# One score matmul per head and block of 32 steps, laid into the score matrix by plain copies

## The chip, the cores and the metric

The kernel runs on one core of one Trainium2 chip. The metric is the device time of one execution in microseconds (us). The version before the change took 1008.17 us, the median of three runs (1007.17 to 1009.46 us).

## The reference

The reference chains three parts. First a linear attention with decay: for each of 4 batches and 8 heads a 48 x 48 state is carried over 768 steps,

```python
cur = einsum('bhd,bhe->bhde', u * k_t, v_t)
y_t = einsum('bhd,bhde->bhe', r_t, state + cur)
state = w_t[..., None] * state + einsum('bhd,bhe->bhde', k_t, v_t)
```

Its output, 3072 tokens of 384 values, goes through a gated feed-forward layer, (sigmoid(x Wg) * (x Wv)) Wo with 1536 hidden units, and that through a second one, mish(x Wi) Wo2 with 2048 hidden units. Everything is float32 with a tight tolerance, so each large product is made of three float16 matmuls (high times high, high times low, low times high).

## The kernel before

**The attention.** Time is cut into blocks of C = 32 steps, and two blocks make a pair; there are 24 blocks (`j`) and 12 pairs (`p`). Inside a block the recurrence becomes a 32 x 32 score matrix per head: the entry (s, t) is the key of step s times the receptance (`r`) of step t, with the decays of the steps between them. The block's output is scores times values plus the decayed `r` times the state that the block starts from.

- `fine(p)` makes the scores inside groups of eight steps, on GpSimd (POOL) and VectorE (DVE), and leaves `r`, `k` and `w` scaled by the decays inside each group.
- `coarse(p, cells)` makes the scores between the four groups of eight of a block. It transposes `k`, `r` and `w` into KD, RD and WD (L573, L567, L580; one tile holds all 32 heads of both blocks), and lets TensorE (PE) form the scores in two levels (L602). The first level, 64 matmuls with 32 x 24 outputs, takes every group's keys against the receptances of the groups from 1 on; then KD's first group and RD's groups 1 and 3 are multiplied by one group's decay each (three `scaled`, L612), and the second level, 64 matmuls with 16 x 16 outputs, writes again over the places where groups 0 and 1 meet groups 2 and 3. A fourth `scaled` prepares RD for the product with the state. The tile X gets the fine scores by a transpose (L618), and `merge` lays the coarse scores over them by one predicated copy with a mask (L625).
- `keys(p)` prepares the keys for the state, transposed into KT (L661).
- `step(j)` multiplies scores and values, and RD and state, into one PSUM tile `yp` (L687), splits it into float16 parts (L204, L207), sends them transposed to `xt`, and updates the state: decay (L763), outer products `kp` (L790), join (L801).

The PSUM tiles `lp` (scores), `yp` and `kp` share three banks of 2 KB each in rotation (`next_at`): a tile can be written once the tile three allocations earlier has been read.

**The feed-forward layers.** `gate(p, f)` and `out1(p, c, part)` are the first layer, on the 256 tokens of a pair: 18 matmuls of 256 columns per `gate` (L835), whose result is multiplied by its sigmoid on ScalarE (ACT) and DVE (L846, L851, L863, L866), and 9 per `out1` part (L899). `h_unit` and `out2` are the second layer (L1020, L1065), which starts when the attention is over. The weights arrive as raw 64-bit words and are decoded to two float16 parts by ACT, DVE and POOL (`decode_early` and `decode`: L275, L286, L297, L300, L351, L362, L375): those of the first layer in the first 130 us, `wi` and `wp` of the second around 535 to 620 us.

**What sets the order.** All work is added as tasks to a `Plan`, with an engine (or several to choose from), an estimated cost and the keys it reads and writes. `Plan.run` is a list scheduler: it keeps a clock per engine by these costs, ranks tasks by how late they may be, and writes each engine's instructions in the order that comes out. Tasks marked `burst` (the small attention matmuls) are kept at least SPACE = 1.9 apart by that clock. On the chip every engine runs its queue in order and waits on semaphores, so a late result on one engine holds everything that stands behind the waiting instruction.

Of the kernel before, what the change touches and what calls it, by code (L numbers as in the profile page):

```python
# [19 lines left out]
NP = NJ // 2  # L20
BH = B * H
HG = BH // 2
DP = 32
BLK = C * (DH + DP + DH)
DM = H * D
KC = DM // 128
# [125 lines left out]
def mixer_moe_kernel(  # L152
# [12 lines left out]
    nc = tc.nc  # L165
# [27 lines left out]
    mask = ap.tile([128, 2, C], F32, name="mask")  # L193
# [202 lines left out]
    xp = {}  # L396
    rd = {}
    kd = {}
    wd = {}
    lps = {}  # L400
# [154 lines left out]
    def coarse(p, cells):  # L555

        R, K, W = (("blk", p % 2, i) for i in range(3))
        RD, KD, WD, X = ("RD", p % 2), "KD", ("WD", p % 2), ("X", p % 2)
        bank = next_at()

        def window(o, step, n):
            v = blk[p][:, o : o + step]
            return bass.AP(v.tensor, v.offset, [list(v.ap[0]), [step, n], [1, 32]])

        def flip_r(e):
# [24 lines left out]

        def level(n, part):
            for i in range(8 * part, 8 * part + 8):
                for e in range(2):
                    for g in range(2):
                        o = 64 * g + 32 * e
                        x = HG * e + i
                        gs = slice(64 * g, 64 * g + 64)
                        if n == 8:
                            m, out, rhs = C, lps[p][o : o + 32, i, 8:], rd[p][gs, x, 8:]
                        else:  # L600
                            m, out, rhs = 16, lps[p][o : o + 16, i, 16:], rd[p][gs, x, 16:]
# [4 lines left out]
        def level8(e):  # L606
            lps[p] = pp.tile([128, HG, C], F32, tag=f"at{bank[1]}", name=f"lp{p}")
            level(8, 0)

        def scaled(e, t, w):  # L610
            shape = [128, BH, t.shape[-1]]
            engines[e].tensor_tensor(  # L612
                out=t, in0=t, in1=w.unsqueeze(2).to_broadcast(shape), op=ALU.mult
            )

        def flip_a(e):
            xp[p] = ap.tile([128, BH, C], F32, tag=f"X{p % 2}", name=f"X{p}")
            nc.vector.transpose(  # L618
                out=xp[p].rearrange("p x t -> p t x"),
                in_=A[:, :1024].rearrange("p (t s) -> p t s", s=C),  # L620
            )

        def merge(e):
            full = [128, 2, HG, C - 8]
            nc.vector.copy_predicated(  # L625
                out=xp[p].rearrange("p (e i) t -> p e i t", e=2)[:, :, :, 8:],
                mask=mask[:, :, 8:].bitcast(U32).unsqueeze(2).to_broadcast(full),
                data=lps[p][:, :, 8:].unsqueeze(1).to_broadcast(full),
            )

        attn("dve", 2.0, flip_k, [K], [KD])
        attn("dve", 2.0, flip_r, [R], [RD])
        attn("dve", 1.9, flip_w, [W], [WD])
        attn("pe", 0.7, level8, [RD, KD], [bank], burst=True)
        attn("pe", 0.7, lambda e: level(8, 1), [RD, KD], [bank], burst=True)
        both = {"dve": 0.8, "pool": 1.05}
        attn(both, 0, lambda e: scaled(e, kd[p][:, :, :8], wd[p][:, 1]), [WD], [KD])
        attn(both, 0, lambda e: scaled(e, rd[p][:, :, 24:], wd[p][:, 2]), [WD], [RD])
        attn(both, 0, lambda e: scaled(e, rd[p][:, :, 8:16], wd[p][:, 0]), [WD], [RD])
        for part in range(2):  # L640
            attn("pe", 0.7, lambda e, n=part: level(16, n), [RD, KD], [bank], burst=True)
        attn({"dve": 1.2, "pool": 1.7}, 0, lambda e: scaled(e, rd[p][:, :, 16:], wd[p][:, 4]), [WD], [RD])
        attn("dve", 2.0, flip_a, [*cells], [X])
        attn("dve", 1.0, merge, [bank, "mask"], [X])

    def keys(p):
        R, K, W = (("blk", p % 2, i) for i in range(3))
# [23 lines left out]
    def step(j):  # L671
        p, e = divmod(j, 2)
        V = ("v", j % 3)
        S, nxt = ([("s", i % 2, x) for x in range(2)] for i in (j, j + 1))
        ybank = next_at()

        def rows_out(part):
            if not part:
                yps[j] = pp.tile([128, 512], F32, tag=f"at{ybank[1]}", name=f"yp{j}")
            for h in range(4 * part, 4 * part + 4):  # L680
                for n in range(2 if j else 1):
                    for b in range(B):
                        g = b // 2
                        gs = slice(64 * g, 64 * g + 64)
                        i = b % 2 * H + h
                        x = HG * e + i
                        nc.tensor.matmul(  # L687
                            yps[j][32 * b : 32 * b + 32, h * D : h * D + D],
                            (rd if n else xp)[p][gs, x, :],
                            (ss if n else vs)[j][gs, i, :],  # L690
                            start=(n == 0),
                            stop=(n == 1 or j == 0),
                        )
# [31 lines left out]
        for part in range(2):  # L725
            attn(
                "pe",
                0.8 * (COLD if j < 4 else 1.0),
                lambda _, part=part: rows_out(part),
                [("X", p % 2), ("RD", p % 2), V, *S],  # L730
                [ybank],
                burst=True,
            )
        xs = ("xs", j % 2)
# [376 lines left out]
            fill=0.0,  # L1111
        )

    def masks(e):

        nc.gpsimd.memset(mask, 0.0)
        for i in range(4):
            m = mask[32 * i : 32 * i + 32, i % 2]
            nc.gpsimd.memset(m, 1.0)
            nc.gpsimd.affine_select(  # L1120
                out=m,
                in_=m,
                pattern=[[8, C // 8], [0, 8]],
                base=0,
                channel_multiplier=-1,
                compare_op=ALU.is_gt,
                fill=0.0,
            )

    add("act", 1.3, lambda e: nc.scalar.preload_act_table(AF.Sigmoid), [], ["table1"])  # L1130
    add("dve", 0.2, consts, [], ["consts"])
    attn("dve", 1.3, lambda e: nc.vector.memset(A, 0.0), [], ["A"])
# [47 lines left out]
            decode(("wp", i), dst, (2, DM), i, slot, ["open"], W2HI, W2LO)  # L1180

    cells = {0: fine(0)}
    attn("pool", 2.0, masks, [], ["mask"])
    tail1(0)
    tail2(0)
    cells[1] = fine(1)
# [86 lines left out]
```

## Time and profile before

| | |
|---|---|
| median of 3 runs | 1008.17 us |
| span of the profiled execution | 1008.4 us |
| PE busy | 937.8 us (93%) |
| DVE busy | 521.2 us (52%) |
| ACT busy | 345.9 us (34%) |
| POOL busy | 309.8 us (31%) |
| share of the chain that ended last, PE | 81% |
| share of it on L602, the score matmuls | 2% |

The chain that ended last is followed back from the last instruction: at each step to what released it, or to the instruction before it on its engine. Busy shares over the whole span hide that the kernel has stretches with different limits: the start with the weight decoding, a long regular stretch in which one pair of attention blocks and one pair of gate work repeat, a transition with the second layer's weights, and the second layer alone. The runs' median and the profiled span differ by 0.02%.

### The profile page before, as it was taken

What the parts mean: (1) busy time and instruction counts of PE and PEld (TensorE: products, weight loads), DVE (VectorE), ACT (ScalarE), POOL (GpSimd) and SP (SyncE); (2) the same over time, 40 slices, a digit from 0 to 9 for tenths busy, and PEclk for the clock granted to TensorE, in tenths of its full rate; (3) what the DMA queues carried; (4) which work ended last, traced back from release to release, by engine and by line L of the source; (5) the groups of instructions that cost most, each with busy time, mean ns of one, the idle gap of its engine ahead of it and who ended that gap; (6) DMA issues with size and microseconds to landing.
All of it is one profiled execution on the core that took longest, in us unless ns stands there. A gap on an engine that the chain in (4) does not pass through costs nothing.

```text
span 1008.4 us, 32823 instructions
## 1 busy us (share of the span) xinstructions
PE 937.8 (93%) x14952; PEld 678.7 (67%) x14952; DVE 521.2 (52%) x830; ACT 345.9 (34%) x692; POOL 309.8 (31%) x324
## 2 busy tenths in 40 slices
PE   0277889999999999999999999999999999999998
PEld 0266778888888888888888787655555555555555
DVE  5898887666675757666679666221111111111110
ACT  3346723222222222222225466443333333333320
POOL 8871383726264553626274111000000000000000
PEclk9998889999999999999999999999999999999999
DMA  9354625131322214132213460010100101000000
GB/s 307 119 167 154 208 75 133 41 86 48 88 41 81 58 62 97 34 87 54 73 36 116 140 202 12 11 45 8 48 8 17 47 8 48 16 9 17 8 16 32
DMA packets 56475, 72.12 MB, mean 72 GB/s; under 512 B 20752, under 2 KB 37648, under 8 KB 56208
## 3 DMA queue, kind: packets, MB, share of 16 engines
q1 hardware_dynamic: 39696, 66.09, 21.7%
q10 hardware_dynamic: 16640, 3.94, 2.1%
q8 instruction: 117, 1.92, 0.8%
q14 instruction: 22, 0.18, 0.1%
HBM read 56.64 MB, written 9.44 MB: 66 GB/s over the span
## 4 chain that ended last, share of the span: by engine, by line
PE 81%; DVE 9%; DMA 5%; ACT 2%; issue 1%; ACTq 1%; SPq 0%; POOL 0%; DVEq 0%
PE gv L835 23%; PE o L1065 19%; PE h L1020 18%; PE o L899 12%; PE yp L687 3%; PE kp L790 3%; PE lp L602 2%; DMA raw_wv<-wv 2%; DMA raw_wg<-wg 1%; DVE A L483 1%; DVE word_wi L286 1%; DMA raw_wp<-wo 1%; DVE word_wi L275 1%; DMA raw_wo<-wo 1%; DVE X L618 1%
## 5 line engine op out<-in xcount | busy, mean ns | idle before, releaser
L1020 PE MATMUL h<-x,wis 128*128 128x512 f16 x864 | 201.5, 379 | 0.0
L835 PE MATMUL gv<-xt,wgs 128*128 128x256 f16 x1296 | 165.6, 275 | 4.3 <-DVE gt L866 3.7
L899 PE MATMUL o<-gt,wos 128*128 128x256 f16 x1296 | 165.5, 273 | 3.2 <-DVE xo L207 3.2
L835 PE MATMUL gv<-xt,wvs 128*128 128x256 f16 x1296 | 166.3, 274 | 0.0
L462 POOL TENSOR_TENSOR blk<-blk 128x384 f32<-128x384 f32 (+1 forms) x144 | 128.8, 907 | 60.2 <-DVE WD L580 31.6
L1020 PEld LDWEIGHTS <-wis 128*128 128x128 f16 x864 | 84.5, 98 | 90.7
L899 PEld LDWEIGHTS <-wos 128*128 128x128 f16 x1296 | 126.6, 98 | 21.7 <-issue 4.1
L835 PEld LDWEIGHTS <-wgs 128*128 128x128 f16 x1296 | 124.2, 98 | 22.0 <-issue 4.8
L835 PEld LDWEIGHTS <-wvs 128*128 128x128 f16 x1296 | 120.8, 98 | 17.9
L846 ACT ACTIVATE sig<-gv 128x256 f32<-128x256 f32 x144 | 55.0, 383 | 226.4 <-PE gv L835 222.9
L1031 ACT ACTIVATE e<-h 128x512 f32<-128x512 f32 x96 | 57.3, 597 | 207.5 <-PE h L1020 207.5
L462 POOL TENSOR_TENSOR pt<-blk 128x384 f32<-128x384 f32 (+1 forms) x96 | 104.9, 1119 | 45.6 <-DMA blk<-rkw 44.1
L851 DVE SCALAR_TENSOR_TENSOR gv<-gv,sig 128x256 f32<-128x256 f32 x144 | 61.9, 431 | 67.7 <-ACT sig L846 67.2
L866 DVE TENSOR_TENSOR gt<-gv,gt 128x256 f16<-128x256 f32 x144 | 60.4, 419 | 36.4 <-ACT gt L863 36.4
L863 ACT CAST gt<-gv 128x256 f16<-128x256 f32 x144 | 53.3, 372 | 72.0 <-DVE gv L851 57.0
L602 PE MATMUL lp<-RD,KD 64*16 64x16 f32 (+1 forms) x3072 | 34.9, 185 | 40.8 <-DVE RD L567 34.1
L602 PEld LDWEIGHTS lp<-RD,KD 64*16 64x16 f32 (+1 forms) x3072 | 30.1, 101 | 50.4 <-DVE RD L567 34.1
L1038 DVE SCALAR_TENSOR_TENSOR wos<-e,wos 128x512 f16<-128x512 f32 x27 | 18.7, 692 | 84.5 <-ACT wos L1034 84.5
L1065 PE MATMUL o<-wps,wgs 128*128 128x384 f16 x324 | 58.5, 326 | 0.0
L1065 PE MATMUL o<-wps,wos 128*128 128x384 f16 x324 | 57.2, 326 | 0.0
L1038 DVE SCALAR_TENSOR_TENSOR wgs<-e,wgs 128x512 f16<-128x512 f32 x27 | 18.7, 692 | 73.8 <-ACT wgs L1034 73.8
L483 DVE TENSOR_REDUCE A<-pt 128x32 f32<-128x768 f32 (+1 forms) x60 | 51.3, 862 | 0.8 <-POOL pt L462 0.8
(91 smaller groups left out, 1065.3 us busy)
## 6 DMA issues: line engine op xcount, KB each, us to landing
v<-vt SPq DMA_DIRECT2D x96, 96.0 KB, 3.0
blk<-rkw SPq DMA_DIRECT2D x22, 384.0 KB, 3.8
raw_wi<-wi SPq DMA_DIRECT2D x8, 768.0 KB, 4.9
raw_wp<-wo SPq DMA_DIRECT2D x8, 768.0 KB, 5.2
blk<-rkw SPq DMA_DIRECT2D x11, 512.0 KB, 4.4
raw_wg<-wg SPq DMA_DIRECT2D x6, 768.0 KB, 4.6
raw_wv<-wv SPq DMA_DIRECT2D x6, 768.0 KB, 5.8
raw_wo<-wo SPq DMA_DIRECT2D x6, 768.0 KB, 5.6
```

Of the source, the lines that this page charges most:

```text
L462: engines[e].tensor_tensor(out=pv, in0=a, in1=b, op=ALU.mult)
L483: nc.vector.tensor_reduce(out=cell(), in_=shape(pts.pop(n)), op=ALU.add, axis=AX.X)
L602: nc.tensor.matmul(out, kd[p][gs, x, :m], rhs, start=True, stop=True, skip_group_check=True)
L835: nc.tensor.matmul(gps[p, f][:, o], w[:, a, kc, fs], xt[p][:, c, kc, :], start=(n == 0), stop=(n == 3 * KC - 1),)
L846: nc.scalar.activation(out=sgs[p, f], in_=gps[p, f][:, 0], func=AF.Sigmoid, scale=1.0 / (SW * SX))
L851: nc.vector.scalar_tensor_tensor(out=gps[p, f][:, 1], in0=gps[p, f][:, 1], scalar=SG / (SW * SX), in1=sgs.pop((p, f)), op0=ALU.mult, op1=A ...
L863: nc.scalar.copy(out=gt[p][:, 0, f], in_=gps[p, f][:, 1])
L866: nc.vector.tensor_tensor(out=gt[p][:, 1, f], in0=gps[p, f][:, 1], in1=gt[p][:, 0, f], op=ALU.subtract,)
L899: nc.tensor.matmul(ops[p, c][:, :NT], wos[:, a, f, cs], gt[p][:, g, f, :], start=(f == 0 and n == 0), stop=(f == NF1 - 1 and n == 2),)
L1020: nc.tensor.matmul(hps[r, f], w2["wi"][:, a, kc, fs], x2[r][:, c, kc, :], start=(n == 0), stop=(n == 3 * KC - 1),)
L1031: nc.scalar.activation(out=es[r, f], in_=hps[r, f], func=AF.Mish, scale=ih)
L1065: nc.tensor.matmul(ops2[r, t][:, :DM], g2[r][f][:, c, tsl], w2["wp"][:, a, f, :], start=(f == 0 and n == 0), stop=(f == NF2 - 1 and n == 2),)
```

## The change

RD becomes wider: 56 columns per head instead of 32 (`RC`), seven groups of eight. Groups 0 to 3 hold what they held; groups 4 and 6 get copies of steps 16 to 23 and 24 to 31 as they leave `fine`, and group 5 gets steps 24 to 31 times one group's decay. `flip_r` fills it by two transposes of half the size (steps 0 to 15 into groups 0 and 1, steps 16 to 31 into groups 4 and 6); two `scaled` then make group 5 from group 6 (256 elements per partition) and groups 2 and 3 from 4 and 5 (512). With that, groups 1 to 6 hold every scaling of `r` that any group of keys needs, and KD is no longer scaled. One matmul per head and block, with all 32 key columns against 48 columns of RD and a 32 x 48 output, gives all scores: 64 per pair instead of 128, in two bursts of 32 (one for each block `e`), each into a PSUM bank of its own. So `coarse` takes two banks of the rotation instead of one.

From the 48 columns the valid ones are laid into X by plain copies from PSUM, `merge(on, e, n)`: for each block `e` and each 32-partition quarter `n` three copies, from 24, 16 and 8 partitions with 8 x 8, 8 x 16 and 8 x 24 elements per partition; a later one overwrites what an earlier one laid on too many rows. That makes 8 tasks and 24 copies per pair, on ACT or DVE as the planner chooses, in place of one predicated copy of 768 elements per partition. The mask and the 9 POOL instructions that made it go away. Last, RD's groups 1 to 3 are multiplied for the product with the state by one `scaled` of 768 elements, after the scores (before: one of 512 after the second level, groups 1 and 3 having been scaled between the levels). `step` waits for the four merges of its own block only. The scratch memory for dynamic DMA is set to 1024 bytes, which makes room for RD's two larger buffers.

```diff
-        bank = next_at()
+        X = [[("X", p % 2, e, n) for n in range(4)] for e in range(2)]
+        banks = [next_at() for _ in range(2)]
...
-            rd[p] = ap.tile([128, BH, C], F32, tag=f"RD{p % 2}", name=f"RD{p}")
-            nc.vector.transpose(
-                out=rd[p].rearrange("p x t -> p t x"), in_=window(0, DH, C)
-            )
+            if not half:
+                out = rd[p][:, :, :16].rearrange("p x t -> p t x")
+            else:
+                out = rd[p].rearrange("p x (b t) -> p b t x", t=8)[:, 4:7:2]
+            nc.vector.transpose(out=out, in_=window(16 * DH * half, DH, 16))
...
-        def level(n, part):
...
+        def scaled(e, to, of, n, w):
+            engines[e].tensor_tensor(
+                out=rd[p][:, :, 8 * to : 8 * (to + n)],
+                in0=rd[p][:, :, 8 * of : 8 * (of + n)],
+                in1=wd[p][:, w].unsqueeze(2).to_broadcast([128, BH, 8 * n]),
...
+        def scores(e):
+            lps[p, e] = pp.tile([128, 8, RC - 8], F32, tag=f"at{banks[e][1]}", name=f"lp{p}_{e}")
+            for i in range(8):
+                for q in range(2):
                     for g in range(2):
-                        o = 64 * g + 32 * e
-                        x = HG * e + i
+                        o = 64 * g + 32 * q
+                        x = HG * e + 8 * q + i
...
                         nc.tensor.matmul(
-                            out, kd[p][gs, x, :m], rhs, start=True, stop=True, skip_group_check=True
+                            lps[p, e][o : o + 32, i], kd[p][gs, x], rd[p][gs, x, 8:], start=True, stop=True
                         )
...
-        def merge(e):
-            full = [128, 2, HG, C - 8]
-            nc.vector.copy_predicated(
...
+        def merge(on, e, n):
+            put = nc.scalar.copy if on == "act" else nc.vector.tensor_copy
+            xs = slice(HG * e + 8 * (n % 2), HG * e + 8 * (n % 2) + 8)
+            for a, c in ((2, 40), (1, 24), (0, 0)):
+                rs = slice(32 * n, 32 * n + 8 * (a + 1))
+                t = 8 * (a + 1)
+                put(out=xp[p][rs, xs, t:], in_=lps[p, e][rs, :, c : c + C - t])
...
+        both = {"dve": 0.55, "pool": 0.9}
+        attn(both, 0, lambda e: scaled(e, 5, 6, 1, 2), [WD], [(*RD, 2)])
+        attn({"dve": 0.85, "pool": 1.35}, 0, lambda e: scaled(e, 2, 4, 2, 1), [WD, (*RD, 2)], [(*RD, 1)])
+        parts = [(*RD, n) for n in range(3)]
+        for e in range(2):
+            attn("pe", 0.85, lambda _, e=e: scores(e), [*parts, KD], [banks[e]], burst=True)
+        attn("dve", 2.0, flip_a, [*cells], X[0] + X[1])
+        for e in range(2):
+            for n in range(4):
+                attn({"act": 0.8, "dve": 0.9}, 0, lambda on, e=e, n=n: merge(on, e, n), [banks[e]], [X[e][n]])
+        attn({"dve": 1.2, "pool": 1.9}, 0, lambda e: scaled(e, 1, 1, 3, 0), [WD], [(*RD, 1)])
```

The order on PE around the scores of pair 8, in the regular stretch, before. A row is an instruction by its line, with output and inputs (`gv7_4` is gate 4 of pair 7, `o16_1` a part of the first layer's output, `kp16_0` the outer products and `yp16` the output of block 16), its size and, behind an x, how many stand in a row.

```order
L602 MATMUL lp8_7133<-RD8_6794,KD8_6738 32x24 x32
...
L835 MATMUL gv7_4_7171<-xt7_6673,wgs_88 128x256
...
L899 MATMUL o16_1_7184<-gt6_6153,wos_90 128x256
...
L602 MATMUL lp8_7133<-RD8_6794,KD8_6738 16x16 x32
...
L790 MATMUL kp16_0_7368<-v16_6083,KT_92 32x48 x32
...
L687 MATMUL yp16_7431<-v16_6083,X8_6671 32x48 x4
```

And the same place on PE after the change.

```order
L611 MATMUL lp8_0_6805<-RD8_6418,KD8_6529 32x48 x32
...
L837 MATMUL gv7_4_6843<-xt7_6284,wgs_88 128x256
...
L901 MATMUL o16_1_6863<-gt6_5865,wos_90 128x256
...
L611 MATMUL lp8_1_6877<-RD8_6418,KD8_6529 32x48 x32
...
L792 MATMUL kp16_0_6947<-v16_5744,KT_92 32x48 x32
...
L689 MATMUL yp16_7011<-v16_5744,X8_6595 32x48 x4
```

Before, four `lp` bursts of 32 stand there (two of each size), with one or two pieces of 9 gate or output matmuls between them; after, two. In both orders the outer products `kp16_0` come before `yp16`. After the change they stand four pieces of 9 and the burst `lp8_1` behind `lp8_0`, and three banks in rotation give `kp16_0` the bank of `lp8_0`.

DVE at the same place, before: the last scaling of RD and the predicated copy.

```order
L866 TENSOR_TENSOR gt7_7038<-gv7_3_7096,gt7_7038 128x256
L612 TENSOR_TENSOR RD8_6794<-RD8_6794,WD8_6857 128x32x8 x2
L851 SCALAR_TENSOR_TENSOR gv7_4_7171<-gv7_4_7171,sig_7249 128x256
L866 TENSOR_TENSOR gt7_7038<-gv7_4_7171,gt7_7038 128x256
L851 SCALAR_TENSOR_TENSOR gv7_5_7238<-gv7_5_7238,sig_7306 128x256
L866 TENSOR_TENSOR gt7_7038<-gv7_5_7238,gt7_7038 128x256
L612 TENSOR_TENSOR RD8_6794<-RD8_6794,WD8_6857 128x32x16
L625 COPY_PREDICATED X8_6671<-mask_94,lp8_7133 128x32x24
```

DVE at the same place, after.

```order
L853 SCALAR_TENSOR_TENSOR gv7_3_6767<-gv7_3_6767,sig_6838 128x256
L628 COPY X8_6595<-lp8_0_6805 24x8x8
L628 COPY X8_6595<-lp8_0_6805 16x8x16
L628 COPY X8_6595<-lp8_0_6805 8x8x24
...
L868 TENSOR_TENSOR gt7_6710<-gv7_3_6767,gt7_6710 128x256
L483 TENSOR_REDUCE A_91<-pt_6779 128x16
L628 COPY X8_6595<-lp8_1_6877 24x8x8
...
L853 SCALAR_TENSOR_TENSOR gv7_4_6843<-gv7_4_6843,sig_6945 128x256
L803 TENSOR_TENSOR s17_6465<-kp16_0_6947,s17_6465 128x384
```

Six copies follow `lp8_0` on DVE and six `lp8_1`; ACT has as many, in front of and behind the cast of `gv7_3`. In pairs 3 to 9 the copies are split 12 and 12, and all scaling of RD stands on POOL, where DVE had three of the four. In pairs 0 to 2 ACT has 48 copies and DVE 24, and DVE two of the scalings (512 and 768 elements; before, three of 256, and two more decays of the state); in pair 11 ACT has 15 and DVE 9, and POOL all scalings.

## Rows read from the trace of the kernel before

**Rows 1.** Stretches: us; busy PE, PEld, DVE, ACT, POOL (x instructions); clock; DMA.
```profile
0.00:137.00 137.00, 74.94 (x2193) 61.78 (x2197) 114.51 (x177) 65.80 (x119) 87.14 (x100) 0.92 0.57 181
...
534.00:625.00 91.00, 85.83 (x1314) 71.89 (x1313) 67.70 (x104) 54.92 (x101) 23.27 (x13) 1.00 0.43 129
...
137.00:534.00 397.00, 396.97 (x9364) 339.88 (x9354) 272.49 (x454) 97.32 (x257) 199.40 (x212) 1.00 0.26 68
```

**Rows 2.** The chain that ended last, one period: start us, us, what.
```profile
259.47 2.95 PE gv L835 x27
...
305.20 2.95 PE gv L835 x27
...
316.01 0.98 PE gv L835 x9
316.99 0.67 PE lp L602 x50
317.67 1.09 PE gv L835 x9
...
322.48 0.62 PE lp L602 x51
323.10 1.09 PE gv L835 x9
...
330.75 0.81 PE yp L687 x64
331.56 1.09 PE gv L835 x9
```

**Rows 3.** Groups by form: PE matmuls of attention: form, count, busy us, mean ns.
```profile
L602 PE MATMUL lp<-RD,KD 64*32 64x24 f32 x1536 | 18.1, 192 | 34.9 <-DVE RD L567 34.1 <-DVE WD L580 0.8
...
L687 PE MATMUL yp<-s,RD 64*32 64x48 f32 x1472 | 40.0, 212 | 1.6 <-DVE s L801 1.6
```

**Rows 4.** Groups by form on ACT, DVE and POOL.
```profile
L204 ACT ACTIVATE xo<-o 128x256 f16<-128x256 f32 x36 | 13.8, 383 | 11.9 <-PE o L899 11.9
L204 ACT ACTIVATE xs<-yp 128x384 f16<-128x384 f32 x24 | 11.7, 490 | 31.2 <-PE yp L687 31.2
L207 DVE SCALAR_TENSOR_TENSOR xo<-o,xo 128x256 f16<-128x256 f32 x36 | 15.1, 418 | 4.2 <-ACT xo L204 3.5
L207 DVE SCALAR_TENSOR_TENSOR xs<-yp,xs 128x384 f16<-128x384 f32 x24 | 13.1, 546 | 0.9 <-ACT xs L204 0.9
L612 DVE TENSOR_TENSOR RD<-RD,WD 128x256 f32<-128x256 f32 x20 | 13.1, 688 | 11.6 <-PE lp L602 11.6
L612 DVE TENSOR_TENSOR RD<-RD,WD 128x512 f32<-128x512 f32 x9 | 11.0, 1222 | 0.0
L612 POOL TENSOR_TENSOR RD<-RD,WD 128x512 f32<-128x512 f32 x3 | 3.2, 1065 | 5.2 <-PE lp L602 5.2
L625 DVE COPY_PREDICATED X<-mask,lp 128x768 f32<-128x768 uint32 x12 | 12.0, 999 | 0.0
L763 DVE TENSOR_TENSOR s<-s,WD 128x384 f32<-128x384 f32 x11 | 7.3, 667 | 0.0
```

**Rows 5.** Waits of PE, 40 to 137 us: who for whom, us in total, times, longest.
```profile
PE yp L687 <- DVE X L625: 5.9, 2, 3.2
PE kp L790 <- issue: 5.7, 3, 3.5
```

**Rows 6.** The chain that ended last, in the transition.
```profile
552.64 0.77 DVE RD L612
...
553.74 0.91 DVE RD L612
...
560.78 2.05 DVE RD L612
562.83 0.94 DVE X L625
...
563.81 0.88 PE yp L687 x64
```

More of the change, by code (lines that the diff above doesn't have):

```diff
@@ L23 @@
 DP = 32
+RC = 56
 BLK = C * (DH + DP + DH)
@@ L192, in mixer_moe_kernel @@
     U = ap.tile([128, DH], F32, name="U")
-    mask = ap.tile([128, 2, C], F32, name="mask")
     engines = {"dve": nc.vector, "pool": nc.gpsimd}
@@ L557, in coarse @@
         R, K, W = (("blk", p % 2, i) for i in range(3))
-        RD, KD, WD, X = ("RD", p % 2), "KD", ("WD", p % 2), ("X", p % 2)
-        bank = next_at()
+        RD, KD, WD = ("RD", p % 2), "KD", ("WD", p % 2)
+        X = [[("X", p % 2, e, n) for n in range(4)] for e in range(2)]
+        banks = [next_at() for _ in range(2)]
         def window(o, step, n):
@@ L563, in window, with flip_r @@
             return bass.AP(v.tensor, v.offset, [list(v.ap[0]), [step, n], [1, 32]])
-        def flip_r(e):
-            rd[p] = ap.tile([128, BH, C], F32, tag=f"RD{p % 2}", name=f"RD{p}")
-            nc.vector.transpose(
-                out=rd[p].rearrange("p x t -> p t x"), in_=window(0, DH, C)
-            )
+        def flip_r(e, half):
+            if p not in rd:
+                rd[p] = ap.tile([128, BH, RC], F32, tag=f"RD{p % 2}", name=f"RD{p}")
+            if not half:
[3 more added lines that the diff above has]
+            nc.vector.transpose(out=out, in_=window(16 * DH * half, DH, 16))
         def flip_k(e):
@@ L589, in flip_w @@
                 )
-        def level(n, part):
-            for i in range(8 * part, 8 * part + 8):
-                for e in range(2):
+        def scaled(e, to, of, n, w):
[3 more added lines that the diff above has]
+                in1=wd[p][:, w].unsqueeze(2).to_broadcast([128, BH, 8 * n]),
+                op=ALU.mult,
+            )
+        def scores(e):
+            lps[p, e] = pp.tile([128, 8, RC - 8], F32, tag=f"at{banks[e][1]}", name=f"lp{p}_{e}")
+            for i in range(8):
+                for q in range(2):
                     for g in range(2):
-                        o = 64 * g + 32 * e
-                        x = HG * e + i
+                        o = 64 * g + 32 * q
+                        x = HG * e + 8 * q + i
                         gs = slice(64 * g, 64 * g + 64)
[L598 to L601, printed above, removed]
                         nc.tensor.matmul(
-                            out, kd[p][gs, x, :m], rhs, start=True, stop=True, skip_group_check=True
+                            lps[p, e][o : o + 32, i], kd[p][gs, x], rd[p][gs, x, 8:], start=True, stop=True
                         )
[L606 to L614, printed above, removed]
         def flip_a(e):
@@ L621, in flip_a @@
             )
-        def merge(e):
-            full = [128, 2, HG, C - 8]
-            nc.vector.copy_predicated(
[L626 to L629, printed above, removed]
+        def merge(on, e, n):
[5 more added lines that the diff above has]
+                put(out=xp[p][rs, xs, t:], in_=lps[p, e][rs, :, c : c + C - t])
@@ L631, in coarse @@
         attn("dve", 2.0, flip_k, [K], [KD])
-        attn("dve", 2.0, flip_r, [R], [RD])
+        attn("dve", 1.1, lambda e: flip_r(e, 0), [R], [(*RD, 0), (*RD, 1)])
+        attn("dve", 1.1, lambda e: flip_r(e, 1), [R], [(*RD, 2)])
         attn("dve", 1.9, flip_w, [W], [WD])
[L634 to L644, printed above, removed]
+        both = {"dve": 0.55, "pool": 0.9}
@@ L673, in step @@
         V = ("v", j % 3)
+        X = [("X", p % 2, e, n) for n in range(4)]
+        RD = [("RD", p % 2, n) for n in range(2)]
         S, nxt = ([("s", i % 2, x) for x in range(2)] for i in (j, j + 1))
@@ L688, in rows_out @@
                             yps[j][32 * b : 32 * b + 32, h * D : h * D + D],
-                            (rd if n else xp)[p][gs, x, :],
+                            (rd if n else xp)[p][gs, x, :C],
                             (ss if n else vs)[j][gs, i, :],
@@ L729, in step @@
                 lambda _, part=part: rows_out(part),
-                [("X", p % 2), ("RD", p % 2), V, *S],
+                [*X, *RD, V, *S],
                 [ybank],
@@ L1112, in unit @@
         )
[L1114 to L1128, printed above, removed]
     add("act", 1.3, lambda e: nc.scalar.preload_act_table(AF.Sigmoid), [], ["table1"])
@@ L1182, in mixer_moe_kernel @@
     cells = {0: fine(0)}
-    attn("pool", 2.0, masks, [], ["mask"])
     tail1(0)
@@ L1261 @@
     }
-    nc = bacc.Bacc("TRN2", target_bir_lowering=False, num_devices=1)
+    nc = bacc.Bacc(
+        "TRN2", target_bir_lowering=False, num_devices=1, dynamic_dma_scratch_size=1024
+    )
     args = [
```

## Prediction

> **What bounds the kernel now.** I read busy time by stretch first, because the shares over the whole span mix four regimes [rows 1]. [...] In the transition, 534 to 625, PE waits some 5 us; after that the second layer is PE alone. [...]
>
> The second view is the chain that ended last, in one period of the long stretch [rows 2]. The reader is to see that it is PE without a break, and what a burst of small matmuls costs in it: its own piece, and 0.11 us by which the piece of 9 gate matmuls behind it is longer (1.09 for 0.98). A first-level score burst is 0.67 + 0.11 = 0.78 us, a second-level one 0.62 + 0.11 = 0.73, a `yp` burst 0.81 + 0.11 = 0.92. The third view gives the shapes [rows 3]: `yp` from RD is K = 64, 32 weight columns, 48 moving columns in float32, on the same four tiles of the array. That is exactly the new score matmul, so its price need not be guessed.
>
> **The change part by part.**
>
> *PE in the long stretch.* Per pair two bursts of each level go, 2 x (0.78 + 0.73) = 3.02 us, and two of the new shape come, 2 x 0.92 = 1.84. That is 1.18 us less per pair. The score bursts of pairs 3 to 10 lie between 137 and 534 us, 8 pairs: 9.4 us. Two bounds, since no score burst of this size is in the trace: were the price set by the number of matmuls alone, the new bursts would cost 2 x 0.78 and the gain 8 x 1.46 = 11.7 us; were it set by the moving columns alone (48 for 24), 4 x 0.78 = 3.12, a loss of 0.8 us. The `yp` row is the same operation, so I take 9.4.
>
> [...] The bursts show about 12 ns per matmul instruction (0.78 us for 64 of them, two to a float32 matmul). [...]
>
> *The copies.* A copy from PSUM costs, by the splitting of `yp` and `o`, 490 ns for 384 elements and 383 for 256 on ACT, and 546 and 418 on DVE [rows 4]: 0.84 and 1.0 ns per element on about 165 ns. Copies of 64, 128 and 192 elements are then some 0.22, 0.28 and 0.33 us: 0.83 us per merge task on ACT, 0.87 on DVE. Partition counts of 8 to 24 are not in the trace. Ends: 24 copies at 0.165 us each, 4 us per pair, and 24 at the 999 ns of the predicated copy, 24 us. I take the line through the two points, 12 copies on each engine: ACT +3.3 us per pair, DVE +3.5. DVE gives up the predicated copy (1.0) and, in pairs 3 to 9, three scalings (0.69, 0.69, 1.22), so its load hardly grows; ACT goes from some 11 to some 14 us of a period of 45. What hides them is the PE stretch itself: neither engine is near its limit there.
>
> [...] ACT's 490 ns at 384 elements is what one long copy costs. [...]
>
> *The waits that the change adds.* `kp` of the first block now takes the bank of `lp_0` and so waits for its four merges. Behind it in PE's queue stand the gates and `yp`. From the end of `lp_0` it comes after two pieces of 9, `lp_1`, and two pieces: 1.09 + 0.98 + 0.81 + 1.09 + 0.98 = 4.95 us. In that time ACT and DVE each lay two merges, 1.7 us, behind at most a sigmoid, a product or a reduction. So there are about 2 to 3 us of slack. `yp` needs RD's last scaling, on POOL (512 elements 1065 ns [rows 4], so 768 some 1.6), after `lp_1`; four pieces and `kp` stand between. Cost nothing, as long as this cover holds.
>
> *The transition.* Pair 11's scores stand among the decoding of `wi`, and there the chain runs through DVE [rows 6]: three scalings, 0.77 + 0.91 + 2.05, and the predicated copy, 0.94, before `yp`. These 4.7 us leave DVE; three merge tasks, 2.6, come. Between a gain of 3.3 us (2.1 on DVE and 1.2 on PE) and a loss of 1.5 us (the last scaling, now on POOL among the weights' subtractions, arrives late) I take a gain of 1.0, since other DVE work fills part of the room.
>
> *The start.* Pairs 0 to 2 lie where DVE is 84% busy. It gets 8 merge tasks, 7.0 us, for three predicated copies, 3.0, and scalings of 512 and 768 elements (1.22 and, by the same slope, 1.75) for three of 256 (2.1): +4.9 us, less two decays at 0.67 [rows 4], +3.6. ACT gets 16 tasks, 13 us on 66, in the queue that decodes the weights. On the other side PE waited 5.9 us for merged X and 5.7 on issue in `kp` [rows 5], two rounds of scaling between PE and the others become one, and the mask is gone from POOL. Ends: all the added DVE work and a third of that again for ACT, +5; most of the wait for X won back, -4. I take +1.5.
>
> *Sum.* -9.4 - 1.0 + 1.5 = -8.9 us on a span of 1008.4. The median of the runs, 1008.17, is the span within 0.02%, so the time becomes 1008.2 - 8.9 = 999.3 us.
>
> **The rivals.**
>
> *The start eats half.* DVE, at 84%, and ACT's in-order queue push the decoding and everything behind it by 5 us, and the transition gives nothing: 1008.2 - 9.4 + 5 = 1003.8. For it: DVE's load there. Against it: PE's 5.9 us of waits for X.
>
> *The start gains too.* The start wins 4 and the transition 3.3: 1008.2 - 9.4 - 7.3 = 991.5. For it: one round of scaling less on a path PE waited on. Against it: DVE has more to do there, not less.
>
> *No gain on PE.* The burst goes by its moving columns: a loss of 0.8, with the start's 1.5 and the transition's 1.0, 1009.5. The `yp` row speaks against it.
>
> *The merges come late (slower).* Place: `kp` of the first block waiting for `lp_0`'s bank in each of the 8 periods, all of PE's queue behind it. If a tiny copy costs as much as the predicated copy, 1.0 us, six in a row are 6 us on each engine behind about 1.5 of other work: 7.5 against 4.95, 2.5 us a period, +20 against -9.4, so 1008.2 + 10.6 + 0.5 = 1019. It decides from a merge task of about 1.7 us (no stall up to there); at 2.3 the gain is gone. The row's line gives 0.85, half of that.
>
> *The bursts don't shrink.* Excluded by the order, which has two bursts of 32 for four.
>
> **How the numbers follow.** My forecast 0.62, alone with a range of 995 to 1003; the start eats half 0.15; the start gains too 0.08; no gain 0.06; late merges 0.09. What can be told from no change is about 0.2%, 2 us. Faster by more than that (below 1006.2): the first three, 0.85; within: most of the fourth, 0.06; slower: the fifth, 0.09. The range that holds 8 in 10 takes in the forecast, the start's loss and half of its gain: 993 to 1006.
>
> **What would show it.** Right: the period of the long stretch falls from 45.73 us (259.47 to 305.20, the same place in successive periods [rows 2]) to about 44.5, PE stays busy all of it, an `lp` piece in the chain reads 0.81 with 1.09 behind it, and copies read 0.2 to 0.35 us. Wrong: waits of `kp` for ACT or DVE copies in the long stretch (late merges); a `lp` piece near 1.4 (no gain); the first saturated microsecond of PE moved from 137 to 142 or to 133 (the start).

## The result and the profile after

The changed kernel takes 1012.59 us (median of 4 runs, 1010.85 to 1013.97) against 1007.67 of the kernel before (4 runs): ratio 1.0051, 95% interval 1.0034 to 1.0068. It is half a per cent slower. The prediction was 999.3 us, 993 to 1006, with 0.85 on faster: wrong in sign and outside its range.

Where it went is read by the start of the same gate matmuls in both traces (first matmul of a pair's gates, before against after, each counted from its span's start). At pair 2, the end of the start, after is 0.54 us late; at pair 10, the end of the regular stretch, 1.15; at the second layer's first matmul, 2.85, and the spans end 2.85 apart. So the start cost 0.5, the stretch 0.6 and the transition 1.7, and the second layer is unchanged. The medians differ by 4.9 us and not by 2.85, mostly because the profiled execution of before was a long one: times lie 1.7 us above spans (the after execution whose span is 1011.3 took 1013.02), so a span of 1008.4 stands for about 1010.1, 2.4 above the median. Where those 2.4 us lie is not shown.

The page of after: busy time of each engine, then two groups of line, operation and shape (busy us, mean ns, idle before).

```profile
PE 929.9 (92%) x13416; PEld 672.2 (66%) x13416; DVE 528.8 (52%) x936; ACT 383.8 (38%) x855; POOL 317.7 (31%) x322
...
L611 PE MATMUL lp<-RD,KD 64*32 64x48 f32 x1536 | 23.3, 216 | 37.0 <-POOL RD L596 37.0
...
L628 ACT COPY X<-lp 24x64 f32<-24x64 f32 x162 | 41.4, 255 | 33.2 <-DVE X L628 25.5
```

The stretches of [rows 1] again, in the same columns. In the long one PE is no longer busy throughout, 389.26 of 397 where it was 396.97; the waits in the next view name 7.4 of the 7.7 us. The second row is the transition: its granted clock is 0.96, where before had 1.00.

```profile
137.00:534.00 397.00, 389.26 (x8367) 334.17 (x8359) 283.88 (x537) 121.57 (x361) 210.66 (x222) 1.00 0.25 68
...
534.00:625.00 91.00, 85.02 (x1184) 72.30 (x1182) 65.19 (x110) 57.16 (x115) 17.27 (x10) 0.96 0.43 129
```

PE's waits in the long stretch (who for whom, us in total, times, longest). Before it had none there.

```profile
PE yp L689 <- DVE s L803: 3.5, 4, 1.3
PE o L901 <- DVE xo L207: 3.3, 5, 0.9
PE yp L689 <- DVE RD L596: 0.6, 1, 0.6
```

The chain that ended last, half a period (start us, us, what), against [rows 2]:

```profile
317.89 0.81 PE lp L611 x64
318.70 1.09 PE gv L837 x9
...
320.77 0.81 PE lp L611 x64
...
329.43 0.81 PE yp L689 x64
330.24 1.10 PE gv L837 x9
...
331.37 0.39 ACT sig L848
331.76 1.46 ACTq L723
...
333.31 1.22 ACTq L723
...
334.57 0.38 ACT gt L865
...
334.98 0.42 DVE gt L868
335.40 0.86 DVE A L483
336.26 0.48 DVE s L803
...
336.78 0.79 PE yp L689 x54
```

The reader is to see two things. The new score burst costs 0.81 with 1.09 behind it, exactly the forecast. And the chain leaves PE: from 331.4 to 334.5 it stands in ACTq, ACT's own instruction queue, which is issuing the two DMA transposes of `xt` (L723); behind them wait ACT's cast of the next gate, DVE's subtraction that needs the cast, a reduction and the state's join (`s`, L803), and for the join PE's next `yp` burst. The same place in ACT's timeline (start us, us, instruction, idle before it and what ended that):

```profile
331.43 3.10 ACTq L723 DMA_TRANSPOSE xt<-xs  x2
334.57 0.37 ACT L865 CAST gt<-gv 128x256 f16<-128x256 f32 x1 [2.83 <-DMA xt<-xs]
```

The releaser named there is the transposes' issue: ACT had been free for 2.83 us with the cast next in its queue.

The transition loses twice. PE's longest wait there, and its part of the chain (start us, us, what):

```profile
PE o L901 <- DVE xo L207: 4.4, 1, 4.4
```

```profile
572.55 6.02 DMA xt<-xs
...
578.77 4.64 DMA raw_wp<-wo
...
584.31 0.38 ACT xo L204
...
584.72 0.43 DVE xo L207
...
585.19 2.08 PE o L901 x9
587.27 3.71 PE gv L837 x18
```

PE waits 4.4 us for the `xo`, and then runs 27 matmuls in 5.79 us, where 27 took 2.95 in the chain of before [rows 2]. From 584 to 591 us the granted clock is 0.52 (0.99 from 578 to 584, 1.00 from 591 to 595). So the wait is followed by 2.8 us that no view of waits shows.

The copies by form (count, busy us, mean ns): 201 to 309 ns on ACT and 223 to 357 on DVE, near the forecast (0.22 to 0.33).

```profile
L628 ACT COPY X<-lp 8x192 f32<-8x192 f32 x54 | 16.7, 309 | 1.7
L628 DVE COPY X<-lp 8x192 f32<-8x192 f32 x42 | 15.0, 357 | 1.4
...
L628 ACT COPY X<-lp 24x64 f32<-24x64 f32 x54 | 10.9, 201 | 29.8 <-DVE X L628 25.5 <-PE lp L611 3.2 <-DVE X L617 0.5
...
L628 DVE COPY X<-lp 24x64 f32<-24x64 f32 x42 | 9.4, 223 | 27.8 <-ACT X L628 26.4 <-PE lp L611 1.1
```

But the two engines don't lay them side by side. One bank's four merges in the timeline: each waits for the other engine's.

```profile
318.77 0.83 ACT L628 COPY X<-lp 24x64 f32<-24x64 f32 x3 [0.40 <-PE lp L611]
319.63 0.92 DVE L628 COPY X<-lp 24x64 f32<-24x64 f32 x3 [0.98 <-ACT X L628]
320.58 0.83 ACT L628 COPY X<-lp 24x64 f32<-24x64 f32 x3 [0.98 <-DVE X L628]
321.44 0.96 DVE L628 COPY X<-lp 24x64 f32<-24x64 f32 x3 [0.90 <-ACT X L628]
```

A bank's merges take 3.6 us, and not the 1.7 that the prediction counted. Over the whole program DVE's copies wait 26.4 us for ACT's, in 31 waits, and ACT's 25.5 for DVE's, in 22. Whether two engines could read one bank without the turns is not shown: no run here tries it.

Last, DVE's queue around the held cast, two pairs after the chain above, in the order in which the program puts it (instruction, tile written, tiles read). Before:

```
504 L618 STREAM_TRANSPOSE X9_7556<-A_91 128x32x32
505 L801 TENSOR_TENSOR s17_6843<-kp16_1_7561,s17_6843 128x384
...
509 L866 TENSOR_TENSOR gt7_7038<-gv7_8_7528,gt7_7038 128x256
```

After:

```
585 L868 TENSOR_TENSOR gt7_6710<-gv7_6_7045,gt7_6710 128x256
586 L803 TENSOR_TENSOR s17_6465<-kp16_1_7134,s17_6465 128x384
```

Before, the gate product that sits behind the transposes' issue (`gv7_8`) came after the join of the state; in after the held product (`gv7_6`) comes just ahead of it; in the pair of the chain a reduction stands between the two. With two score bursts fewer in front, the pair's first `yp` now starts 20.5 us into the period (counted from its first gate matmul), where it was 25.6, and its transposes are issued at 25.5 instead of 30.0. Before paid the same hold (40 issues, median 1.22 us) and nothing on PE waited for what stood behind it.

### The profile page after: what moved, and what is told of

The parts are those of the page before. It is cut to its first block, busy times and chain, and to the rows that moved or that the text cites. A ratio compares the mean times of both kernels' runs of the same rounds, so it can differ in the third digit from the quotient of the medians.

```text
span 1011.3 us, 30037 instructions
## 1 busy us (share of the span) xinstructions
PE 929.9 (92%) x13416; PEld 672.2 (66%) x13416; DVE 528.8 (52%) x936; ACT 383.8 (38%) x855; POOL 317.7 (31%) x322
## 4 chain that ended last, share of the span: by engine, by line
PE 81%; DVE 7%; DMA 5%; ACT 4%; issue 1%; ACTq 1%; POOL 1%; SPq 0%; DVEq 0%
PE gv L837 23%; PE o L1067 19%; PE h L1022 18%; PE o L901 13%; PE yp L689 3%; PE kp L792 3%; PE lp L611 2%; DMA xt<-xs 1%; ACTq L723 1%; DMA raw_wo<-wo 1%; DVE A L483 1%; POOL wos L300 1%; DVE X L628 1%; ACT X L628 1%; DMA raw_wv<-wv 1%
## 5 line engine op out<-in xcount | busy, mean ns | idle before, releaser
L837 PE MATMUL gv<-xt,wgs 128*128 128x256 f16 x1296 | 167.9, 277 | 11.5 <-DVE gt L868 11.5
L837 PEld LDWEIGHTS <-wvs 128*128 128x128 f16 x1296 | 123.2, 99 | 18.3
L462 POOL TENSOR_TENSOR blk<-blk 128x384 f32<-128x384 f32 (+1 forms) x144 | 124.9, 885 | 26.1 <-DVE KD L577 12.4
L462 POOL TENSOR_TENSOR pt<-blk 128x384 f32<-128x384 f32 (+1 forms) x96 | 107.1, 1141 | 66.8 <-DMA blk<-rkw 62.6
L596 POOL TENSOR_TENSOR RD<-RD,WD 128x256 f32<-128x256 f32 (+2 forms) x33 | 35.1, 1064 | 95.7 <-PE lp L611 50.1
L611 PE MATMUL lp<-RD,KD 64*32 64x48 f32 x1536 | 23.3, 216 | 37.0 <-POOL RD L596 37.0
L628 ACT COPY X<-lp 24x64 f32<-24x64 f32 x162 | 41.4, 255 | 33.2 <-DVE X L628 25.5
```

Of the source, the lines that this page charges most:

```text
L462: engines[e].tensor_tensor(out=pv, in0=a, in1=b, op=ALU.mult)
L611: nc.tensor.matmul(lps[p, e][o : o + 32, i], kd[p][gs, x], rd[p][gs, x, 8:], start=True, stop=True)
L628: put(out=xp[p][rs, xs, t:], in_=lps[p, e][rs, :, c : c + C - t])
L837: nc.tensor.matmul(gps[p, f][:, o], w[:, a, kc, fs], xt[p][:, c, kc, :], start=(n == 0), stop=(n == 3 * KC - 1),)
```

## The experiments

Theory A: the loss in the long stretch is the issue of two transposes in ACT's queue, which now stands ahead of what PE needs. Rival B: the copies themselves, in turns, make PE wait. Two more came up on the way: C, it takes the hold together with the place of the `yp` bursts, which the engine of RD's last scaling sets; D, it takes the turns. All runs in one table: ratio to the kernel before with its interval, and lateness in us against the trace of before at the first gate matmul of pair 2, of pair 10, and at the second layer. Each lateness is of one execution. In experiment 2 the queues are those of before up to the first DMA transpose, and yet it is 1.9 late at pair 1, so differences of 2 us at the start are not told apart.

| kernel | ratio | pair 2 | pair 10 | second layer |
|---|---|---|---|---|
| changed | 1.0051 [1.0034, 1.0068] | +0.5 | +1.2 | +2.8 |
| 1 e1_send_sp | 0.9953 [0.9935, 0.9971] | +0.3 | -7.6 | -10.2 |
| 2 e5_before_send_sp | 0.9998 [0.9981, 1.0015] | +1.3 | +1.9 | 0.0 |
| 3 e3_send_cost | 1.0016 [1.0002, 1.0029] | +0.7 | -6.9 | -0.6 |
| 4 e8_send_cost_early | 0.9978 [0.9963, 0.9994] | +1.4 | -5.7 | -2.8 |
| 5 e4_before_send_cost | 1.0007 [0.9990, 1.0025] | -1.3 | -1.2 | -2.9 |
| 6 e9_one_sp | 1.0307 [1.0280, 1.0333] | +1.3 | +23.6 | +28.8 |
| 7 e11_three | 1.0602 [1.0556, 1.0649] | 0.0 | +45.7 | +51.0 |
| 8 e2_third | 0.9978 [0.9964, 0.9993] | -4.0 | -4.3 | -4.7 |
| 9 e6_sp_bank_each | 0.9982 [0.9964, 1.0001] | +9.3 | -0.3 | -2.2 |
| 10 e7_sp_act | 0.9965 [0.9944, 0.9986] | +5.8 | -3.8 | -7.5 |
| 11 e10_sp_act_late | 0.9915 [0.9884, 0.9945] | +0.4 | -9.2 | -13.3 |
| 12 e12_act_late | 0.9896 [0.9871, 0.9921] | +0.8 | -8.6 | -12.7 |
| 13 e13_last_scaling_dve | 1.0035 [1.0018, 1.0052] | +1.1 | -1.7 | +0.6 |
| 14 e14_act_late_pool | 1.0030 [1.0003, 1.0058] | +0.7 | +2.1 | -2.3 |

**1, transposes issued by SyncE.**

```
-                nc.scalar.dma_start_transpose(
+                nc.sync.dma_start_transpose(
-            attn("act", 0.15, send, [*reads, *room], new, lat=2.8)
+            attn("sp", 0.15, send, [*reads, *room], new, lat=2.8)
```

> The changed kernel with its DMA transposes issued from SP's queue instead of ACT's; the written order of PE, DVE and ACT up to gate (11, 5) is otherwise that of the changed kernel. Theory A (two transpose issues, 3.1 us, stand in ACT's queue ahead of a cast; DVE's subtraction waits for that cast and the state's join and the split of the output stand behind it, so PE waits some 1.25 us a period): the period of the long stretch falls from 45.80 to about 44.6 us, PE waits there nearly vanish, time about 1012.6 - 8 x 1.2 = 1003 us (1001 to 1005). Theory B (the copies, which ACT and DVE lay in turns, 7.4 us a pair instead of 3.5 side by side, hold both queues): the period stays 45.8, time 1011 to 1013.

Measured, as A says: 1003.1 us, period 44.80 us in nearly every pair (changed: mostly 45.77; before 45.74), stretch -8.0, transition -2.6. PE's waits for DVE in the stretch are gone; this is all that is left:

```profile
PE kp L792 <- issue: 0.4, 1, 0.4
```

**2, the same edit in the kernel before**, as a control.

> The kernel before, with the attention's transposes issued by SyncE instead of ScalarE; PE's order is unchanged. Theory A (what the change lost is the 3.1 us issue of two transposes that came to stand ahead of needed work): the stretch of before showed no PE wait, so nothing is to be had there: gate (10,0) within 0.6 us of before's, and at the second layer's start 0 to -2.5 us, so 1005 to 1008 us. Rival: the issue on ScalarE costs any kernel of this shape the same, and the gain of the changed kernel with SyncE had nothing to do with the change: stretch -7 to -8 us, 998 to 1000 us.

Measured: +0.6 in the stretch, no change in all. So the gain of 1 is one that the change had lost, not one to be had anyway.

**3, 4 and 5, the issue on ACT but with an honest price for the planner** (2.6 us and 0.4 latency for 0.15 and 2.8): everywhere, for the first ten pairs alone (there 0.35 of latency), and in the kernel before. The edit of 3 and 5:

```
-            attn("act", 0.15, send, [*reads, *room], new, lat=2.8)
+            attn("act", 2.6, send, [*reads, *room], new, lat=0.4)
```

> The changed kernel with one number of the plan altered: the transposes' issue costs the planner 2.6 on ACT instead of 0.15 (latency 0.4 instead of 2.8). The transposes stay on ACT, but the state's join now stands ahead of the subtraction that waits for the cast. Theory A: period about 44.6, time about 1003 (1000 to 1006, since start and transition are ordered anew too). Theory B: period 45.8, time 1010 to 1013.

> The changed kernel with the planner's cost of the transposes' issue set to 2.6 for the first ten pairs alone and left at 0.15 for the last two. The kernel with 2.6 everywhere gained 7.6 us by the end of the stretch and gave 6.4 back around the last pairs. If it gave them back because the number changed the queues of the last two pairs: stretch -6.5 as there, the rest like the changed kernel's (+1.7 us), second layer at -5 us, 1004 us. If the loss comes with anything that arrives there early (weights of the second layer not ready): second layer again at -0.2 us, 1009 us.

> The kernel before with the same altered number (2.6 on ACT for the transposes' issue). Control for the last one. Theory A: PE had no waits in the long stretch before, so its period stays 45.73 and the time 1007.7, give or take 2 for the newly ordered start and transition. If this kernel gains as much as e3 does against the changed one, the number and not the change is what e3 shows.

Measured: 3 won 7.6 us in the stretch and 4 won 7.1, by reordering alone; in before it won nothing (+0.2). But 3 gave 6.4 us back in the transition and 4 gave 2.9. Experiment 4 lost less, though neither of its two stories fits: the second layer started at -2.8, between -5 and -0.2. In both the granted clock from 534 to 625 us is 0.96. What the other order costs around the last pairs is not settled. The time of 3, 1009.4 us, is above the 1000 to 1006 that A had said.

**6 and 7, one and three issues on ACT for two**, with PE's, DVE's and POOL's order as in the changed kernel.

```
-                nc.scalar.dma_start_transpose(
+                (nc.scalar, nc.sync)[i].dma_start_transpose(
```

```
-            for i in range(2):
+            for i in (0, 1, 1):
                 nc.scalar.dma_start_transpose(
```

> The changed kernel with every engine's order kept as it is, but the second of the two transposes of a step issued by SyncE, so that ScalarE's queue is held by one issue (1.2 to 1.6 us) instead of two (3.10 us). Theory A: PE stalls by what the hold exceeds some slack by; with 1.25 us of stall per pair for 3.10 us of hold the slack is about 1.85 us, and a hold of 1.6 us is inside it: no stall is left, the stretch gains what was forecast or nearly (-8 us at gate (10,0) against before), 1002 to 1004 us. Rival: the stall goes with the length of the hold from zero: half of it stays, stretch -3.5 us, 1007 to 1009 us. If the issue isn't the cause at all: 1012 us as the changed kernel.

> The changed kernel, order as it is, with the second transpose of each step issued twice on ScalarE (the same data to the same place): the queue is held for some 4.3 to 4.7 us instead of 3.10. Theory A: PE's stall grows by the added hold, 1.2 to 1.6 us in each of the 8 pairs of the stretch, gate (10,0) at +10 to +14 us against before instead of +1, 1021 to 1027 us in all. If the issue isn't the cause: 1012 to 1014 us.

Measured: 7 was slower by much more than expected, and 6, meant to halve the hold, was 3% slower. The chain of 6 shows why: in it ACT's transpose is issued 0.06 us after SyncE's has landed (343.81 + 2.29, then 346.16).

```profile
343.81 2.29 DMA xt<-xs
346.16 1.20 ACTq L723
```

At the chain's next such place 3.80 us of landing stand in front of an issue of 1.20, with 0.07 us between. So the hold got longer: ACT's cast behind the first of them waited 4.00 us, where it waited 2.83 in the changed kernel. The expectation of 6 did not count the landing; as a test it still gives a point of the curve. Idle time of ACT before the cast, between 137 and 530 us, in the changed kernel, in 6 and in 7 (behind the last bar: total idle, and what ended it):

```profile
L865 ACT CAST gt<-gv 128x256 f16<-128x256 f32 x106 | 39.4, 372 | 100.6 <-DVE gv L853 60.9 <-DMA xt<-xs 33.0 <-DVE KD L577 6.4
```

```profile
L865 ACT CAST gt<-gv 128x256 f16<-128x256 f32 x100 | 37.2, 372 | 129.3 <-DVE gv L853 64.0 <-issue 54.6 <-DVE KD L577 10.5
```

```profile
L865 ACT CAST gt<-gv 128x256 f16<-128x256 f32 x95 | 35.3, 372 | 172.0 <-issue 97.1 <-DVE gv L853 74.7
```

33.0, 54.6 and 97.1 us of hold go with +0.6, +22.3 and +45.8 us of stretch. The order being the same, A's direction is shown: the hold grows by 21.6 and 64.1, the stretch by 21.7 and 45.1. It is no clean measure of the hold, for the granted clock from 137 to 534 us is 0.97 in 6 and 7 and 1.00 in the changed kernel (0.974 and 0.983 over the whole execution). From 175 to 560 us PE waits for the join 7 times in each: 18.3 us in 6, the longest 3.7, and 31.5 in 7, the longest 5.5. An estimate from the shares of the stretch: 0.03 of 397 us, so up to some 12 us of either growth, may be the clock's.

**8, a third of the copies** (the last copy of each merge only; part of the scores is left out), order as it is.

```
-                for a, c in ((2, 40), (1, 24), (0, 0)):
+                for a, c in ((0, 0),):
```

> The changed kernel with only the last copy (8 partitions, 8 x 24 elements) of each merge's three, in the same order on every engine; so part of the scores between groups of eight (keys of the second and third group) is left out of the result. The turns of ACT and DVE shrink from 7.4 us a pair to about 3. Theory A: PE's waits in the long stretch stay, period 45.6 to 45.8, time 1010.5 to 1012.5. Theory B: period about 44.6, time about 1003.

Measured: the start is 4.5 us shorter than the changed kernel's, the stretch -0.3, period 45.75 in most pairs, and the join still makes PE wait, longer than all else:

```profile
PE yp L689 <- DVE s L803: 4.0, 5, 1.1
```

B falls for the stretch: the length of the copies is not what PE waits for there. At the start it is worth some 4 us, which A had left out: it had said 1010.5 to 1012.5 us, and 1005.7 came.

**9, 10 and 11, SyncE's issue and no turns**: one bank's merges on ACT and the other's on DVE; all on ACT; all on ACT from pair 3 on. Each has the edit of 1 too; those of 9 and 11 for the copies:

```
-                attn({"act": 0.8, "dve": 0.9}, 0, lambda on, e=e, n=n: merge(on, e, n), [banks[e]], [X[e][n]])
+                attn(({"act": 0.8}, {"dve": 0.9})[e], 0, lambda on, e=e, n=n: merge(on, e, n), [banks[e]], [X[e][n]])
```

```
-                attn({"act": 0.8, "dve": 0.9}, 0, lambda on, e=e, n=n: merge(on, e, n), [banks[e]], [X[e][n]])
+                attn({"act": 0.8, "dve": 0.9} if p < 3 else {"act": 0.8}, 0, lambda on, e=e, n=n: merge(on, e, n), [banks[e]], [X[e][n]])
```

> The changed kernel with the transposes issued by SyncE, and the four copies tasks of the first bank all on ScalarE, those of the second all on VectorE, so that no task waits for the other engine's. If the turns only lie beside other work once ScalarE's queue is free: the stretch like that of the kernel with SyncE alone (-8 us against before, period 44.7 us), the start like it or up to 3 us shorter (leaving out two of three copies took 4.2 us off the start), so 999.5 to 1003 us. If the turns still cost in the stretch: period under 44.5 us and another 1 to 3 us less there.

> The changed kernel with the transposes issued by SyncE and all eight copies tasks on ScalarE: 8 x 0.83 = 6.6 us on one queue instead of 7.4 us in turns. If only the turns matter, it is like the kernel with one bank on each engine in the stretch. If a queue that holds copies ahead of the gates' ScalarE steps makes PE wait, as the transposes' issue did, it loses against the kernel with SyncE alone: 1 us per pair at most, 1003 to 1010 us; at the start, where ScalarE is busy with weights, 0 to +4 us.

> The changed kernel with both transposes on SyncE, the copies in turns on ScalarE and VectorE for the first three pairs (as in the kernel with SyncE alone, whose start was 0.5 us above before's) and all on ScalarE from the fourth on (that had 1.18 us less per pair in the stretch, as forecast, but a start 6 us above before's). If start and stretch are separate: start +0.5, stretch -9, transition -2.5 to -3.7, second layer at -11 to -12.5 us, 1000 to 1003 us. If the turns of the kernel with SyncE alone cost nothing any more, it is like that one, second layer at -10 us, 1003 us.

Measured: all three have a period of 44.57 us from pair 2 to pair 9, every pair: 1.17 under before, the forecast's 1.18. So with ACT's queue free of the issue the turns, and the order that comes with them, cost 0.23 us a pair. 9 and 10 lost 9 and 6 us at the start, more than expected; 11, which leaves the start alone, reached -13.3 us at the second layer, 996.96 us in the median, where 1000 to 1003 had been expected.

**12, copies on ACT from pair 3 on, transposes left on ACT** (the second edit above in the changed kernel).

> The changed kernel with the transposes left on ScalarE, and the copies from the fourth pair on all on ScalarE, so without turns: the fourth corner beside the changed kernel (turns, hold), the one with SyncE alone (turns, no hold) and the one with SyncE and ScalarE's copies (neither). Theory A: the hold of some 3 us is still ahead of the cast and the join that PE needs, so most of the stall stays: stretch between -3 and +1 us against before at gate (10,0), 1008 to 1013 us. If the turns were enough by themselves: period 44.6 us, stretch -9 us, 1000 to 1003 us.

Measured: 996.78 us, period 44.57 in all pairs but one. A alone had said 1008 to 1013 and falls: the hold is still there and costs nothing. Here is its place, in ACT's timeline:

```profile
324.17 2.68 ACTq L723 DMA_TRANSPOSE xt<-xs  x2
327.59 0.38 ACT L848 ACTIVATE sig<-gv 128x256 f32<-128x256 f32 x1 [3.45 <-PE gv L837]
```

ACT had nothing to do: its next sigmoid waited 3.45 us for PE, and the hold lies inside that. In PE's order the two `yp` bursts now stand ahead of the first `kp` burst, where the changed kernel has `kp` first, so the transposes are issued one slot earlier. The order moved for a reason that is not the turns: with its copies gone from DVE, the planner put RD's last scaling on DVE (from pair 3 to 10) instead of POOL, where it takes 1.49 us.

**13 and 14 cross the two**: turns kept and the last scaling on DVE; no turns (as 12) and the last scaling on POOL. Both have the issue on ACT.

```
-        attn({"dve": 1.2, "pool": 1.9}, 0, lambda e: scaled(e, 1, 1, 3, 0), [WD], [(*RD, 1)])
+        attn({"dve": 1.2, "pool": 1.9} if p < 3 else {"dve": 1.2}, 0, lambda e: scaled(e, 1, 1, 3, 0), [WD], [(*RD, 1)])
```

> The changed kernel with one engine choice taken away: from the fourth pair on the last scaling of RD stands on VectorE and not on GpSimd. Copies in turns and transposes on ScalarE stay. By it the two yp bursts of a pair's first half stand ahead of the first kp burst in TensorE's order, as in the kernel with ScalarE's copies. Theory C (the stall needs both the hold of ScalarE's queue and that place of the yp bursts, which the last scaling on GpSimd sets): period 44.6 to 44.8 us, gate (10,0) at -7 to -9 us, 996 to 1001 us. If the turns of the copies are needed for the stall and enough with the hold (rival D): period 45.7 us, 1008 to 1013 us.

> The kernel that has its copies on ScalarE alone from the fourth pair on, with the last scaling of RD forced back onto GpSimd there: no turns, but the first kp burst again ahead of the yp bursts, as in the changed kernel. Theory C: the stall is back, period 45.3 to 45.8 us, gate (10,0) between -3 and +1 us, 1005 to 1012 us. Rival D (no turns, no stall): period 44.6 us, 996 to 1000 us, as without the force.

Measured, 14: as C says, and a little more (+2.1 at pair 10, where it had said -3 to +1). Without turns, but with `kp` first again, the old stall is back, period 45.4 to 46.7, with PE's two waits of the changed kernel (between 137 and 530 us):

```profile
PE o L901 <- DVE xo L207: 4.4, 8, 1.0
PE yp L689 <- DVE s L803: 3.2, 5, 1.4
```

Measured, 13: C fails in the number. The time, 1012.1 us, lies where D had put it, but D's reason fails with 14 and with what PE waits for here. The stall at the join is gone, but another has come, of `yp` for the scaling. Its chain:

```profile
319.01 0.23 DVE X L628
...
319.96 0.21 ACT X L628
...
320.83 0.24 DVE X L628
...
323.17 1.26 DVE RD L596
...
324.48 0.80 PE yp L689 x56
```

The copies go in turns, the scaling stands behind them in DVE's queue, and `yp` waits for it (5.2 us in 7 waits, period 44.7 to 46.0). So this version pays by the turns, the changed kernel by the hold, and 12, which has neither the copies on DVE nor the hold in that place, by nothing.

## Why the prediction was wrong, point by point

*PE in the long stretch, -9.4.* Right, and hidden. Burst and piece are 0.81 and 1.09; where nothing is late the period is 44.57, and kernel 12's stretch is -9.4 us (+0.8 to -8.6).

*The waits that the change adds, at nothing.* This is the step that failed. It followed `kp` and `yp` to the merges and to RD's last scaling on POOL, and found cover for both. It did not ask what the `yp` that moves carries along. Behind `yp` come the splitting of its output and then two DMA transposes, whose issue holds ACT's queue for some 3 us (3.10 in the chain); the step shows no row on them. Moved to the new slot, they stand ahead of a cast, its subtraction and the state's join. Against the period of 44.57 every pair but one loses some 1.2 us or more (mostly 45.77), 10.0 us over the stretch: all that was forecast there and a little more. Without the hold 8.6 of them come back (1); most of the rest goes with the turns (1 against 11). Shown by 1 and 2 (take the hold away), by 12 (keep it, in a free place) and 14 (bring the place back).

*The copies, at nothing.* Their duration was right within 10%. That two engines would lay two merges each in 1.7 us was wrong: a bank takes 3.6 us in turns. In the long stretch that costs little by itself (0.23 us a pair in 1, with its order); it decides in 13, and at the start the copies cost some 4 us (8). The rival of late merges at `kp` did not come: the turns were within its slack of 4.95 us.

*The start, +1.5.* +0.5 in the traces, inside its ends, and not to be told from +1.5 by one execution of each; 9 and 10 show how wide it is, up to +9.3 for another deal of the same copies.

*The transition, -1.0.* +1.7. In 11 and 12, where the copies leave DVE too, it is -4.1, beyond the bound of -3.3. In the changed kernel 4.4 us go to PE's wait for DVE's part of an `xo` and 2.8 to the lower clock behind it, for which the sum had no term. The transition goes with that clock: -3.7 to -4.5 in 10, 11, 12 and 14, whose granted clock from 534 to 625 us is 1.00; -1.9 and -2.6 at 0.98 (9 and 1); -0.4 to +6.4 at 0.96 (the changed kernel, 3, 4, 8 and 13). What the wait itself comes from, by the chain a weight load behind the landing of two transposes, no run took apart.

*The base.* The sum took the span of 1008.4 for the median's time, but times lie 1.7 above spans. The forecast was counted from the median in the end, so this moved no number of it.

The sum was off by 11.75 us in the traces (+2.85 for -8.9): 10.0 in the stretch, 2.7 in the transition, less 0.95 at the start. A rival with this mechanism was not among those named; the one slower case had another place and 20 us.

## What to carry to other kernels

A step that moves in the plan takes its whole tail along. List every instruction that the tail puts into an in-order queue, DMA issues by the time that they hold the queue and not by the planner's price, and ask what then stands behind them and who waits for that; a hold that cost nothing in its old place says nothing of the new one. When a saving in a saturated engine does not appear, compare the period first, then look for the first row of the chain that leaves that engine. Here the best version (12, 0.9896 of before) differs from the slower one by one written engine choice, the copies', and by a second one that the planner made for it.

## What the runs showed that was not expected

- Issuing one DMA transpose of 128 x 384 float16 held the issuing queue 1.2 us or more (1.20 to 2.26 on ACT in the changed kernel, median 1.22; 1.19 to 2.13 on SyncE in experiment 11, median 1.20; two in a row 2.7 to 3.1 in the places shown); the planner's price for two was 0.15.
- In the two places that the chain of experiment 6 shows, ACT's transpose was issued 0.06 and 0.07 us after SyncE's had landed (2.29 and 3.80 us, each with 1.20 of issue behind it): dealing them to two queues made the kernel 3% slower, SyncE's alone made it faster (0.9953).
- In the transition of the changed kernel more was lost than the length of PE's wait: behind 4.4 us of it the granted clock was 0.52 from 584 to 591 us, and 27 matmuls took 5.79 us for 2.95.
- Two engines that copy from one PSUM bank take turns in this program: 0.83 + 0.92 us in a row with 0.9 to 1.0 idle on each.
